# Linear attention in plain float32, its narrow products in 64- and 32-wide parts of TensorE, in a fused attention and gated-MLP kernel

## The chip, the cores and the metric

The program runs on one core of a Trainium2 chip. The time is device microseconds (us) of that core; each time given is the median over several executions, and the profile is of one further execution. The engines are called by the profile's names: PE is TensorE (PEld its weight loads), DVE is VectorE, ACT is ScalarE, POOL is GpSimd, SP is SyncE, which here issues every DMA.

## The reference

Eight batches of eight heads, 576 tokens, head size 64, 128 features. The attention is linear: no softmax over tokens, but a feature map and two products. Its output is the input of a gated MLP without a non-linearity.

```python
def phi(x):                                      # x: b h s d (8, 8, 576, 64)
    proj = np.einsum('bhsd,df->bhsf', x, w_phi)  # w_phi: 64 x 128
    proj = proj - np.max(np.abs(proj), axis=-1, keepdims=True)
    return np.concatenate([np.exp(proj), np.exp(-proj)], axis=-1)   # 256 features
q_p, k_p = phi(q), phi(k)
kv  = np.einsum('bhsf,bhsd->bhfd', k_p, v)
z   = np.sum(k_p, axis=2)
num = np.einsum('bhsf,bhfd->bhsd', q_p, kv)
den = np.einsum('bhsf,bhf->bhs', q_p, z)[..., None] + 1e-06
x   = num / den                                  # as 4608 tokens x 512
out = ((x @ w_a) * (x @ w_b)) @ w_out            # 512 -> 1536 -> 512
```

The MLP's weights arrive as float64 bits and are decoded on the chip.

## The kernel before, in words

**Two number formats.** PE multiplies float32 exactly but slowly, and `F32R`, a rounded float32, fast. Where the kernel wants both it splits a number into `hi + lo`, both F32R, and makes three products (`hi*hi`, `hi*lo`, `lo*hi`; helper `products`, L99). The MLP does this throughout. The attention does it from a certain head pair on; before that it uses plain float32 ("plain" in the code), with thresholds in L38: the k features are plain for the first 9 of 32 pairs, the q features for 2, the sums over k for 11, the numerators for 7.

**Attention.** A unit of work is a pair of heads (4 pairs per batch, 32 in all). Per pair:

- `k_load`, `rest_load` load k and v (512 of the 576 tokens in four chunks of 128; the last 64 tokens of two pairs share one 128-row "rest" tile), and where not plain split them: `ks` (k stacked as hi over lo), `vaug`/`vl`.
- `features` makes the k features for two chunks at a time: product `pk` (L219 plain, L228 split), maximum and subtraction on DVE, two exponentials on ACT, where split also `keh` (ACT) and `kel` (DVE).
- `kv_add` (L286) accumulates v-transposed times features into `kvps`, per chunk and head, 256 columns wide. v has a 65th column of ones, so that row 65 of the result is z. Split: three products, two of 65 and one of 64 weights' columns.
- `k_finish` transposes the result (`pt`, four transposes) into `kvh` (and `kvl`).
- `q_side`, once per head: load q, `pq` (L340) for its features, a maximum over partitions on POOL (`mb`), a subtraction on DVE, two exponentials on ACT, where split `qeh` (ACT) and `qel` (DVE), and `pn` (L364), whose 65 rows are numerator and denominator. They go to DRAM as `xun` and `den`; `reciprocals` turns `den` into `rec` once per batch.

**The MLP** has d_ff 1536 in two passes: pass 0 takes 6 of 12 slices of 128 for 16 blocks of 288 tokens, pass 1 the other 6 for 9 blocks of 512 tokens and adds the stored partial sums. `pa`, `pb` (L515) and `po` (L538) are its products, 216 matmuls per block. `decode` turns the raw weights `raw` into `wh`/`wl` with two ACT and six DVE instructions per weight tile (18 tiles for each pass) by way of two work tiles `wg`, `ws`.

**Order.** `attention_steps` places the stages of every pair in numbered turns (tables L24 to L31). After each turn `due` MLP steps are given out (L35); batch b's blocks may start `BLOCK_LAG` turns after its reciprocals. That is the order of writing; the framework's scheduler then settles the order on each engine. Each engine runs its list strictly in that order. Pass 1 follows when pass 0 is through.

Of the kernel before, what the change touches and what calls it, by code (L numbers as in the profile page):

```python
# [55 lines left out]
@with_exitstack
def tile_kernel(ctx, tc, qT, km, kr, vm, vr, w_phi, w_a, w_b, w_out, out):

# [40 lines left out]
    def products(a, b):  # L99

        if len(a) == 1:
            return [(a[0], b[0])]
        return [(a[0], b[0]), (a[0], b[1]), (a[1], b[0])]

    def attention_consts(a1):
# [18 lines left out]
        vaug = []  # L124
        for i in range(2):
            t = a1.tile([P, NFULL, 2, D + 1], F32R, name=f"vaug{i}")
            nc.vector.memset(t[:, :, :, D : D + 1].bitcast(F32), 1.0)
            vaug.append(t)
        return w2, wh, wl, wk32, wk2, ident, vaug

    def engine(step, b):
        return {"v": nc.vector, "s": nc.scalar}[ENGINES[step][min(b, 2)]]

    def copy(eng, dst, src):
        if eng is nc.scalar:
            eng.copy(dst, src)  # L136
        else:
            eng.tensor_copy(dst, src)

    def split(hi, lo, src, eng_hi, eng_lo):  # L140

        copy(eng_hi, hi, src)
        eng_lo.tensor_tensor(lo, src, hi, op=ALU.subtract)  # L143

    def stack(hi_lo, src, eng_hi, eng_lo):

        copy(eng_hi, hi_lo, src)
        eng_lo.tensor_tensor(hi_lo[D:], src[D:], hi_lo[D:], op=ALU.subtract)  # L148

    def k_load(b, pr, a1, a2, ps, consts, st):  # L150
        vaug = consts[-1]
        u = f"{b}_{pr}"
        i = b * NPAIR + pr
        n = NFULL * P
        if i < PLAIN_K:
            k32 = a1.tile([P, n], F32, tag="ks", bufs=2, name=f"k32_{u}")
            nc.sync.dma_start(k32, km[b, pr])
# [4 lines left out]
        if i < PLAIN_KV:  # L162
            v32 = a1.tile([P, NFULL, 2, D + 1], F32, tag="vl", bufs=2, name=f"v32_{u}")
            nc.vector.memset(v32[:, :, :, D : D + 1], 1.0)
        else:
            v32 = a1.tile([P, NFULL, 2, D], F32, tag="v32", name=f"v32_{u}")
        nc.sync.dma_start(v32[:, :, :, :D], vm[b, pr])
        yield
        st["k", b, pr] = (k32,)
        if i >= PLAIN_K:  # L170
            ks = a1.tile([P, 2, n], F32R, tag="ks", bufs=2, name=f"ks_{u}")
            stack(ks, k32, engine("k_hi", b), engine("k_lo", b))
            st["k", b, pr] = (ks,)
        yield
        st["v", b, pr] = (v32,)
        if i >= PLAIN_KV:
            va = vaug[pr % 2]
            vl = a1.tile([P, NFULL, 2, D + 1], F32R, tag="vl", bufs=2, name=f"vl_{u}")
            split(va[:, :, :, :D], vl[:, :, :, :D], v32, engine("v_hi", b), engine("v_lo", b))
            st["v", b, pr] = (va, vl)  # L180
        yield

    def rest_load(b, g, a1, a2, ps, consts, st):

        u = f"{b}_{g}"
        i = b * NPAIR + 2 * g
        if i < PLAIN_K:
            k32 = a1.tile([P, P], F32, tag="rk32", name=f"rk32_{u}")
            nc.sync.dma_start(k32, kr[b, g])
# [4 lines left out]
        v32 = a1.tile([P, 2, D + 1], F32, tag="rv32", name=f"rv32_{u}")  # L194
        nc.vector.memset(v32[:, :, D : D + 1], 1.0)
        nc.sync.dma_start(v32[:, :, :D], vr[b, g])
        yield
        st["rk", b, g] = (k32,)
        if i >= PLAIN_K:
            ks = a1.tile([P, 2, P], F32R, tag="rk", name=f"rk_{u}")  # L200
            stack(ks, k32, engine("k_hi", b), engine("k_lo", b))
            st["rk", b, g] = (ks,)
        yield
        st["rv", b, g] = (v32,)
        if i >= PLAIN_KV:
            vh = a1.tile([P, 2, D + 1], F32R, tag="rvh", name=f"rvh_{u}")
            vl = a1.tile([P, 2, D + 1], F32R, tag="rvl", name=f"rvl_{u}")
            split(vh, vl, v32, engine("v_hi", b), engine("v_lo", b))
            st["rv", b, g] = (vh, vl)
        yield  # L210

    def features(u, i, k_, c0, n, a2, ps, consts):

# [22 lines left out]
        plain = i < PLAIN_KV  # L236
        shape = [P, 2 * n, 2, F]
        if plain:
            e = a2.tile(shape, F32, tag=f"keh{n}", bufs=n, name=f"ke_{u}")
        else:  # L240
            e = a2.tile([P, 4, 2, F], F32, tag="ke", bufs=1, name=f"ke_{u}")[:, : 2 * n]
# [2 lines left out]
        es = (e,)
        if not plain:
            eh = a2.tile(shape, F32R, tag=f"keh{n}", bufs=n, name=f"keh_{u}")
            el = a2.tile(shape, F32R, tag=f"kel{n}", bufs=n, name=f"kel_{u}")
            split(eh, el, e, engine("ke_hi", i // NPAIR), nc.vector)
            es = (eh, el)
        yield es  # L250
# [23 lines left out]
    def rest_add(b, pr, st):  # L274
        rows = slice(pr % 2 * REST, (pr % 2 + 1) * REST)
        kv_add(b, pr, [v_[rows] for v_ in st["rv", b, pr // 2]], [e_[rows] for e_ in st["re", b, pr // 2]], st)
        yield

    def kv_add(b, pr, vs, es, st):

        left = st["kv_left", b, pr] = st["kv_left", b, pr] - 1
        for j in range(2):
            parts = products(vs, es)
            for n_, (v_, e_) in enumerate(parts):
                width = D if n_ == 2 else D + 1
                nc.tensor.matmul(  # L286
                    st["kv_ps", b, pr][:width, j],
                    v_[:, j, :width],
                    e_[:, j],
                    start=(left == NFULL and j == 0 and n_ == 0),  # L290
                    stop=(left == 0 and n_ == len(parts) - 1),
                    skip_group_check=True,
                )
# [5 lines left out]
    def k_finish(b, pr, a1, a2, ps, consts, st):  # L299
        ident = consts[5]  # L300
        u = f"{b}_{pr}"
        assert st["kv_left", b, pr] == 0
# [3 lines left out]
        pt = pool.tile([P, 4, P], F32, tag=tag, bufs=bufs, name=f"pt_{u}")
        for g in range(4):
            nc.tensor.transpose(pt[:, g, : D + 1], kvT[: D + 1, g, :], ident[: D + 1, : D + 1])
        plain = b * NPAIR + pr < PLAIN_NUM
        kvh = a2.tile([P, 4, D + 1], F32 if plain else F32R, tag="kvh", name=f"kvh_{u}")  # L310
        nc.scalar.copy(kvh, pt[:, :, : D + 1])
        st["kv", b, pr] = (kvh,)
        if not plain:
            kvl = a2.tile([P, 4, D + 1], F32R, tag="kvl", name=f"kvl_{u}")
            nc.vector.tensor_tensor(kvl, pt[:, :, : D + 1], kvh, op=ALU.subtract)
            st["kv", b, pr] = (kvh, kvl)
        yield

    def q_side(b, pr, j, a1, a2, ps, consts, st):
        w2, wh, wl = consts[:3]  # L320
        h = 2 * pr + j
        i = b * NPAIR + pr
        plain_q, plain = i < PLAIN_Q, i < PLAIN_NUM
        u = f"{b}_{h}"
# [311 lines left out]
```

## Time and profile before

| | |
|---|---|
| median of 3 runs | 1301.69 us (1298.23 to 1302.58) |
| the profiled execution | 1299.35 us, its span 1297.6 us |
| granted TensorE clock, mean | 0.991 |
| busy of the span: PE, PEld | 1253.2 us (97%), 1114.9 us (86%) |
| busy: DVE, ACT, POOL | 841.9 (65%), 703.1 (54%), 157.1 us (12%) |
| HBM | 138.8 MB in the DMA queue of the kernel, mean 108 GB/s |

How to read a row of a timeline: start in us from the span's start, duration in us, engine, line, operation, output<-inputs, weights' rows*columns, moving operand, and how many instructions are merged (x4); in brackets the idle time ahead and what ended it. The profile counts records: a plain float32 matmul leaves two, each with a weight load of its own, an F32R one leaves one. Matmuls overlap in their pipeline, so a record's duration is longer than its share of PE's time; the spacing of starts in an unbroken run is what one really costs.

### The profile page before, as it was taken

How to read it: one execution, taken by the hardware profiler on the slowest of the kernel's cores; microseconds unless marked ns; L12 is line 12 of the kernel's file. 1: busy time of each engine (PE TensorE's matmuls, PEld its weight loads, DVE VectorE, ACT ScalarE, POOL GpSimd, SP SyncE). 2: the span in 40 equal slices, each digit the busy share in tenths (PEclk: the TensorE clock that was granted, in tenths of full speed). 3: DMA queues.
4: the chain of work that ended last, by engine and by line, in shares of the span. 5: the costliest groups of instructions: out<-in, count | busy, mean ns of one | idle time of the engine just before them, and what ended most of it. 6: DMA issues, size and time to landing. Idle time of an engine off the chain costs nothing.

```text
span 1297.6 us, 20263 instructions
## 1 busy us (share of the span) xinstructions
PE 1253.2 (97%) x7632; PEld 1114.9 (86%) x7632; DVE 841.9 (65%) x1388; ACT 703.1 (54%) x1471; POOL 157.1 (12%) x70
## 2 busy tenths in 40 slices
PE   7989879999999999999999999999999999999998
PEld 4558659999999999999999899988888888888887
DVE  5999985798998989988973532698323323333322
ACT  5777775788989888988884322443211211211210
POOL 2323211131222222221220000000000000000000
PEclk9999979999999999999999999999999999999999
DMA  8666532443433435344224821243233133133100
GB/s 197 169 179 177 155 100 77 110 114 107 132 102 112 134 82 156 87 123 123 55 80 117 241 83 56 66 155 110 73 114 98 49 114 98 49 114 96 51 33 33
DMA packets 116594, 140.12 MB, mean 108 GB/s; under 512 B 29136, under 2 KB 81872, under 8 KB 116496
## 3 DMA queue, kind: packets, MB, share of 16 engines
q1 hardware_dynamic: 116496, 138.83, 37.4%
q8 instruction: 60, 0.98, 0.3%
q14 instruction: 38, 0.31, 0.1%
HBM read 110.18 MB, written 28.61 MB: 107 GB/s over the span
## 4 chain that ended last, share of the span: by engine, by line
PE 53%; DVE 7%; ACT 2%; issue 2%; DMA 2%; SPq 0%; DVEq 0%; ACTq 0%
PE po L538 17%; PE pb L515 16%; PE pa L515 16%; PE kvps L286 2%; PE pn L364 2%; DVE qs L148 1%; DVE kel L143 1%; DMA rb<-rec 1%; DVE qel L143 0%; DVE kd L231 0%; DVE kd L234 0%; DVE ks L148 0%; PE pq L340 0%; DMA den<-xn 0%; DVE x L492 0%
## 5 line engine op out<-in xcount | busy, mean ns | idle before, releaser
L344 POOL PARTITION_ALL_REDUCE mb<-p x64 | 156.4, 2444 | 512.8 <-ACT p L341 304.0
L515 PE MATMUL pa<-xh,wh_a 128*128 128x288 f32 (+1 forms) x600 | 200.2, 334 | 5.3 <-DVE h L520 3.1
L538 PE MATMUL po<-hh,wl_o 128*128 128x288 f32 (+1 forms) x600 | 195.8, 331 | 7.2 <-DVE wl_o L433 7.0
L515 PE MATMUL pb<-xh,wh_b 128*128 128x288 f32 (+1 forms) x600 | 198.8, 331 | 4.1 <-ACT h L519 4.1
L520 DVE TENSOR_TENSOR h<-pb,h 128x288 f32<-128x288 f32 (+1 forms) x150 | 80.5, 538 | 185.9 <-PE pb L515 185.2
L515 PE MATMUL pa<-xl,wh_a 128*128 128x288 f32 (+1 forms) x600 | 198.8, 331 | 0.0
L538 PE MATMUL po<-hl,wh_o 128*128 128x288 f32 (+1 forms) x600 | 198.2, 332 | 0.1
L515 PE MATMUL pb<-xl,wh_b 128*128 128x288 f32 (+1 forms) x600 | 198.0, 330 | 0.0
L515 PE MATMUL pa<-xh,wl_a 128*128 128x288 f32 (+1 forms) x600 | 197.8, 330 | 0.0
L515 PE MATMUL pb<-xh,wl_b 128*128 128x288 f32 (+1 forms) x600 | 197.4, 329 | 0.0
L538 PE MATMUL po<-hh,wh_o 128*128 128x288 f32 (+1 forms) x600 | 196.2, 333 | 1.0 <-ACT o L541 0.5
L136 ACT CAST hh<-h 128x288 fp32r<-128x288 f32 (+1 forms) x150 | 75.3, 502 | 192.5 <-DVE h L520 189.8
L519 ACT COPY h<-pa 128x288 f32<-128x288 f32 (+1 forms) x150 | 70.2, 469 | 186.3 <-PE pa L515 184.5
L538 PEld LDWEIGHTS po<-hh,wl_o 128*128 128x128 f32 x600 | 113.2, 189 | 16.6 <-DVE wl_o L433 7.3
L515 PEld LDWEIGHTS pa<-xh,wh_a 128*128 128x128 f32 x600 | 113.3, 189 | 15.8 <-DVE h L520 4.2
L515 PEld LDWEIGHTS pb<-xh,wh_b 128*128 128x128 f32 x600 | 112.9, 188 | 14.7 <-ACT h L519 5.9
L538 PEld LDWEIGHTS po<-hh,wh_o 128*128 128x128 f32 x600 | 112.8, 190 | 11.1 <-DVE h L520 0.9
L538 PEld LDWEIGHTS po<-hl,wh_o 128*128 128x128 f32 x600 | 113.9, 190 | 9.0 <-DVE hl L143 0.4
L515 PEld LDWEIGHTS pa<-xh,wl_a 128*128 128x128 f32 x600 | 113.6, 189 | 8.6
L515 PEld LDWEIGHTS pa<-xl,wh_a 128*128 128x128 f32 x600 | 113.4, 189 | 8.8 <-issue 0.2
L515 PEld LDWEIGHTS pb<-xl,wh_b 128*128 128x128 f32 x600 | 113.0, 188 | 8.5 <-issue 0.2
L515 PEld LDWEIGHTS pb<-xh,wl_b 128*128 128x128 f32 x600 | 112.9, 188 | 8.5
(131 smaller groups left out, 2339.2 us busy)
## 6 DMA issues: line engine op xcount, KB each, us to landing
q<-in_qT SPq DMA_DIRECT2D x124, 144.0 KB
k<-in_km SPq DMA_DIRECT2D x55, 256.0 KB
xun<-xn SPq DMA_DIRECT2D x64, 144.0 KB
x<-xun SPq DMA_DIRECT2D x32, 288.0 KB
rb<-rec SPq DMA_DIRECT2D x64, 144.0 KB
part<-o SPq DMA_DIRECT2D x16, 576.0 KB
o<-part SPq DMA_DIRECT2D x9, 1024.0 KB
v<-in_vm SPq DMA_DIRECT2D x32, 256.0 KB
```

The costliest lines, as they stand in the source:

```text
L136: eng.copy(dst, src)
L143: eng_lo.tensor_tensor(lo, src, hi, op=ALU.subtract)
L148: eng_lo.tensor_tensor(hi_lo[D:], src[D:], hi_lo[D:], op=ALU.subtract)
L286: nc.tensor.matmul(st["kv_ps", b, pr][:width, j], v_[:, j, :width], e_[:, j], start=(left == NFULL and j == 0 and n_ == 0), stop=(left == ...
L344: nc.gpsimd.partition_all_reduce(mb, p32, P, bass_isa.ReduceOp.absmax)
L364: nc.tensor.matmul(pn[: D + 1, :HALF], kv_[:, 2 * j + s, :], e_[:, s, tok], **at)
L515: nc.tensor.matmul(acc, w[:, cc * P : (cc + 1) * P], x, start=(k == 0), stop=(k == 3 * NCC - 1))
L519: nc.scalar.copy(h32, pab["a"])
L520: nc.vector.tensor_tensor(h32, pab["b"], h32, op=ALU.mult)
L538: nc.tensor.matmul(acc, w[:, cc * P : (cc + 1) * P], h, start=(k == 0), stop=(k == 3 * NFS[p] - 1))
```

## The change

- `kv_add`, `q_side` and `k_finish` use plain float32 for all pairs; `products`, the hi/lo copies of q, v and of the features, `vaug`, and the table `ENGINES` go. Only the k features stay split, from pair 7 on (before: 9).
- The sums over k: v has 64 columns now, head 0 of a pair goes to PSUM partitions 0 to 63, head 1 to 64 to 127 (columns 0 to 63 and 64 to 127 of the array). z is a product of its own: 32 columns of ones as weights, in one of four 32-column parts, `q = 2c + j`. So per two chunks four 64-column and four 32-column products, 256 columns of features each.
- `k_finish`: two 128-wide transposes, and two products with `pick`, which add up the z rows.
- `q_side` takes a pair at once: one load of 128 rows; `pq` with 64 rows of weights per head, rows 0 to 63 or 64 to 127; `pn` with 64 columns per head; the denominator `pd` as 32-column products, one part per head and half of the tokens.
- `decode`'s work tiles `wg`, `ws` have two buffers in pass 0 (before: one).
- The tables of turns and paces are others.

```diff
-TURNS0, TURNS, PAIRS0 = 5, 4, 7
+TURNS0, TURNS, PAIRS0 = 5, 4, 5
-KV_TURN = 7
-Q_TURNS, Q_STEP = (0, 3, 4, 6, 9), 3
-DECODE_TURN, BLOCK_LAG = 2, 8
-PACE0, PACE, PACE0_UNTIL = 0.65, 0.9, 18
-PLAIN_K, PLAIN_Q, PLAIN_KV, PLAIN_NUM = 9, 2, 11, 7
+KV_TURN = 8
+Q_TURNS = (0, 3, 4, 6, 7, 9, 11)
+DECODE_TURN, BLOCK_LAG = 2, 6
+PACE0, PACE, PACE0_UNTIL = 0.8, 0.9, 24
+PLAIN_K = 7
+QUAD = 32
...
+        ones = a1.tile([P, QUAD], F32, name="ones")
+        nc.vector.memset(ones, 1.0)
+        pick = a1.tile([P, 2, QUAD], F32, name="pick")
+        nc.vector.memset(pick, 0.0)
+        for q in range(4):
+            nc.vector.memset(pick[q * QUAD : q * QUAD + 1, q % 2], 1.0)
...
+        kv_add(b, pr, [(v[:, c0 + c, j], e[:, 2 * c + j], j, 2 * c + j) for c in range(2) for j in range(2)], consts, st)
...
+    def kv_add(b, pr, parts, consts, st, rows=slice(0, P)):
+        ones, ps = consts[4], st["kv_ps", b, pr]
         left = st["kv_left", b, pr] = st["kv_left", b, pr] - 1
-        for j in range(2):
-            parts = products(vs, es)
-            for n_, (v_, e_) in enumerate(parts):
-                width = D if n_ == 2 else D + 1
-                nc.tensor.matmul(st["kv_ps", b, pr][:width, j], v_[:, j, :width], e_[:, j], ...)
+        for i, (v_, e_, j, q) in enumerate(parts):
+            nc.tensor.matmul(ps[j * D : (j + 1) * D, 0], v_, e_.rearrange("p s f -> p (s f)"), **at)
+        for v_, e_, j, q in parts:
+            to = ps[q * QUAD : (q + 1) * QUAD, 1]
+            nc.tensor.matmul(to, ones[rows], e_.rearrange("p s f -> p (s f)"), tile_position=(rows.start, q * QUAD), **at)
...
+        q32 = a2.tile([P, S], F32, tag="q32", name=f"q32_{u}")
+        nc.sync.dma_start(q32, qT[b, 2 * pr : 2 * pr + 2].rearrange("j d s -> (j d) s"))
+        for i, tok in enumerate(toks):
+            pq = [ps.tile([P, 512], F32, tag="att", name=f"pq_{u}_{i}_{j}")[:, :HALF] for j in range(2)]
+            for j in range(2):
+                rows = slice(j * D, (j + 1) * D)
+                nc.tensor.matmul(pq[j], w2[rows], q32[rows, tok], start=True, stop=True)
...
+        for i, tok in enumerate(toks):
+            for s in range(2):
+                for j in range(2):
+                    nc.tensor.matmul(pn[i][j * D : (j + 1) * D], kv[:, s, j], es[j][:, s, tok], **at)
+        for s in range(2):
+            for j in range(2):
+                for i, tok in enumerate(toks):
+                    q = (2 * j + i) * QUAD
+                    at = dict(start=(s == 0), stop=(s == 1), tile_position=(0, q))
+                    nc.tensor.matmul(pd[q : q + QUAD], z[:, s, j], es[j][:, s, tok], **at)
...
-            return pool.tile(shape, dt, tag=kind, bufs=1, name=name)
+            return pool.tile(shape, dt, tag=kind, bufs=2, name=name)
```

Two places show how the instructions stand after scheduling. The first is PE in the middle of the program, where the products of a pair stand among those of the MLP. Before, a head's numerators (`qeh`, `qel` and `kvh`, `kvl` are the hi and lo halves of the q features and of the transposed sums):

```order
L340 MATMUL pq_0_1_3802<-qs_0_3794,wh 128x288
L340 MATMUL pq_0_1_3802<-qs_0_3794,wl 128x288
L364 MATMUL pn_5_0_3857<-qeh_5_3620,kvh_2_3474 65x288 x2
L364 MATMUL pn_5_0_3857<-qel_5_3621,kvh_2_3474 65x288 x2
L364 MATMUL pn_5_0_3857<-qeh_5_3620,kvl_2_3476 65x288 x2
L538 MATMUL po_3_1_4346<-hh_3_0_3751,wh_0_o 128x288
```

and in the changed program the denominators of a pair (`pd`, after its eight `pn`), two chunks of k sums (64 and 32 columns), the rest's sums (64 rows), and the next pair's q products:

```order
L308 MATMUL pd_2_4431<-qe_2_0_4097,kv_2_4253 32x288 x2
L308 MATMUL pd_2_4431<-qe_2_1_4308,kv_2_4253 32x288 x2
L233 MATMUL kvps_3_4311<-ke_3_2_4320,v_4_3_3756 64x256 x4
L237 MATMUL kvps_3_4311<-ke_3_2_4320,ones 32x256 x4
L233 MATMUL kvps_3_4311<-ke_1_r,rv_4_1_3485 64x256 x2
L237 MATMUL kvps_3_4311<-ke_1_r,ones 32x256 x2
L278 MATMUL pq_0_0_0_4466<-q_5_0_4273,w_100 128x288
L278 MATMUL pq_0_0_1_4467<-q_5_0_4273,w_100 128x288
L278 MATMUL pq_0_1_0_4472<-q_5_0_4273,w_100 128x288
L464 MATMUL pa_4_5_4488<-xh_4_0_4069,wh_5_a 128x288
```

The products of different parts now mostly stand behind one another, in runs of four to eight, and the runs of different width follow one another directly.

The second is DVE near the start, while weights are decoded (L427 to L433, later L376 to L382) beside the first pairs. Before:

```order
L427 TENSOR_SCALAR wg_2_a<-wg_2_a 128x512
L428 SCALAR_TENSOR_TENSOR ws_2_a<-raw_2_a,wg_2_a 128x512
L233 TENSOR_REDUCE m_3_2_599<-pk_3_2_596 128x4
L138 CAST qs_7_705<-q_0_7_631 128x576
L429 TENSOR_SCALAR wg_2_a<-ws_2_a 128x512
L234 TENSOR_TENSOR kd_3_2_595<-pk_3_2_596,m_3_2_599 128x512
L148 TENSOR_TENSOR qs_7_705<-q_0_7_631,qs_7_705 64x576
L345 TENSOR_TENSOR p_0_5_545<-p_0_5_545,mb_5_592 128x576
L431 SCALAR_TENSOR_TENSOR wg_2_a<-raw_2_a,wg_2_a 128x512
L432 TENSOR_TENSOR ws_2_a<-ws_2_a,wh_2_a 128x512
L433 TENSOR_TENSOR wl_2_a<-ws_2_a,wg_2_a 128x512
```

and now:

```order
L286 TENSOR_TENSOR p_0_2_1_492<-p_0_2_1_492,mb_2_1_626 128x576
L380 SCALAR_TENSOR_TENSOR wg_3_b<-raw_3_b,wg_3_b 128x512
L376 TENSOR_SCALAR wg_4_a<-wg_4_a 128x512
L191 TENSOR_REDUCE m_0_0_712<-pk_0_0_709 128x4
L381 TENSOR_TENSOR ws_3_b<-ws_3_b,wh_3_b 128x512
L377 SCALAR_TENSOR_TENSOR ws_4_a<-raw_4_a,wg_4_a 128x512
L192 TENSOR_TENSOR kd_0_0_708<-pk_0_0_709,m_0_0_712 128x512
L382 TENSOR_TENSOR wl_3_b<-ws_3_b,wg_3_b 128x512
L378 TENSOR_SCALAR wg_4_a<-ws_4_a 128x512
L380 SCALAR_TENSOR_TENSOR wg_4_a<-raw_4_a,wg_4_a 128x512
L381 TENSOR_TENSOR ws_4_a<-ws_4_a,wh_4_a 128x512
```

The q splits (L138, L148) are gone, and two weights (`3_b`, `4_a`) are decoded interleaved. Ahead of DVE's first MLP instruction (the first `x`, which releases the first `pa`) stand 9 finished weights before and 13 now; ahead of PE's first `pa` stand 200 attention matmuls before and 292 now.

More of the change, by code (lines that the diff above doesn't have):

```diff
@@ L97, in attention_pools @@
         return a1, a2, ps
[L99 to L103, printed above, removed]
     def attention_consts(a1):
@@ L123, in attention_consts, with stack, split @@
         make_identity(nc, ident)
[L124 to L148, printed above, removed]
+        ones = a1.tile([P, QUAD], F32, name="ones")
[4 more added lines that the diff above has]
+            nc.vector.memset(pick[q * QUAD : q * QUAD + 1, q % 2], 1.0)
+        return w2, wk32, wk2, ident, ones, pick
+    def stack(hi_lo, src):
+        nc.scalar.copy(hi_lo, src)
+        nc.vector.tensor_tensor(hi_lo[D:], src[D:], hi_lo[D:], op=ALU.subtract)
+    def split(hi, lo, src):
+        nc.scalar.copy(hi, src)
+        nc.vector.tensor_tensor(lo, src, hi, op=ALU.subtract)
     def k_load(b, pr, a1, a2, ps, consts, st):
-        vaug = consts[-1]
         u = f"{b}_{pr}"
-        i = b * NPAIR + pr
         n = NFULL * P
-        if i < PLAIN_K:
-            k32 = a1.tile([P, n], F32, tag="ks", bufs=2, name=f"k32_{u}")
-            nc.sync.dma_start(k32, km[b, pr])
+        plain = b * NPAIR + pr < PLAIN_K
+        if plain:
+            k_ = a1.tile([P, n], F32, tag="ks", bufs=2, name=f"k32_{u}")
+            nc.sync.dma_start(k_, km[b, pr])
         else:
@@ L161, in k_load @@
                 nc.sync.dma_start(k32[r * D : (r + 1) * D], km[b, pr].rearrange("(j d) s -> d j s", j=2))
[L162 to L167, printed above, removed]
-        yield
[L169 to L180, printed above, removed]
+        v32 = a1.tile([P, NFULL, 2, D], F32, tag="v32", bufs=3, name=f"v32_{u}")
+        nc.sync.dma_start(v32, vm[b, pr])
+        st["v", b, pr] = v32
+        yield
+        if not plain:
+            k_ = a1.tile([P, 2, n], F32R, tag="ks", bufs=2, name=f"ks_{u}")
+            stack(k_, k32)
+        st["k", b, pr] = k_
         yield
@@ L185, in rest_load @@
         u = f"{b}_{g}"
[L186 to L189, printed above, removed]
+        plain = b * NPAIR + 2 * g < PLAIN_K
+        if plain:
+            k_ = a1.tile([P, P], F32, tag="rk32", name=f"rk32_{u}")
+            nc.sync.dma_start(k_, kr[b, g])
         else:
@@ L235, in features @@
         yield
[L236 to L241, printed above, removed]
+        e = a2.tile([P, 2 * n, 2, F], F32, tag=f"ke{n}", bufs=1 + n, name=f"ke_{u}")
         nc.scalar.activation(e[:, :, 0, :], d, AF.Exp)
         nc.scalar.activation(e[:, :, 1, :], d, AF.Exp, scale=-1.0)
[L244 to L250, printed above, removed]
+        yield e
     def k_chunks(b, pr, c0, a1, a2, ps, consts, st):
         u = f"{b}_{pr}"
-        gen = features(f"{u}_{c0}", b * NPAIR + pr, st["k", b, pr][0], c0, 2, a2, ps, consts)
+        gen = features(f"{u}_{c0}", b * NPAIR + pr, st["k", b, pr], c0, 2, a2, ps, consts)
         yield next(gen)
-        es = next(gen)
+        e = next(gen)
         yield
@@ L305, in k_finish @@
         pool, tag, bufs = spare(b, ps)
[L306 to L316, printed above, removed]
@@ L317, in k_finish @@
-        yield
[L319 to L324, printed above, removed]
+        pt = pool.tile([P, 512], F32, tag=tag, bufs=bufs, name=f"pt_{u}")
+        for s in range(2):
+            nc.tensor.transpose(pt[:, s * P : (s + 1) * P], kvT[:, 0, s], ident)
+        nz = 2 * QUAD
+        for s in range(2):
+            to = pt[:, 2 * P + s * nz : 2 * P + (s + 1) * nz]
+            nc.tensor.matmul(to, kvT[:, 1, s], pick.rearrange("p j r -> p (j r)"), start=True, stop=True)
@@ L356, in q_side @@
-        yield
-        parts = [(s, kv_, e_) for kv_, e_ in products(st["kv", b, pr], es) for s in range(2)]
-        xn = a2.tile([P, S], F32, tag="xn", name=f"xn_{u}")
-        for i in range(2):
-            tok = slice(i * HALF, (i + 1) * HALF)
-            pn = ps.tile([P, 512], F32, tag="att", name=f"pn_{u}_{i}")
-            for n_, (s, kv_, e_) in enumerate(parts):
-                at = dict(start=(n_ == 0), stop=(n_ == len(parts) - 1))
-                nc.tensor.matmul(pn[: D + 1, :HALF], kv_[:, 2 * j + s, :], e_[:, s, tok], **at)
-            nc.scalar.copy(xn[: D + 1, tok], pn[: D + 1, :HALF])
```

151 lines of the change are left out of this document (67 added, 84 removed).

## The prediction

> **What bounds the kernel now.** I read the page's head and its shares of the engines, then busy time by stretches, then PE's timeline, because the spacing of starts there gives what each kind of product really costs.
>
> ```profile
> span 1297.6 us, 20263 instructions
> PE 1253.2 (97%) x7632; PEld 1114.9 (86%) x7632; DVE 841.9 (65%) x1388; ACT 703.1 (54%) x1471; POOL 157.1 (12%) x70
> 0.00:94.00 94.00, 78.06 (x340) 48.93 (x340) 76.92 (x139) 63.69 (x136) 29.22 (x18) 1.00 0.71 185
> 0.00:200.00 200.00, 169.36 (x849) 123.83 (x850) 170.94 (x298) 139.03 (x298) 52.43 (x27) 0.95 0.60 161
> 200.00:700.00 500.00, 493.03 (x3736) 477.56 (x3735) 430.63 (x672) 416.70 (x895) 104.65 (x43) 1.00 0.38 104
> 850.00:1298.00 448.00, 443.86 (x1967) 367.49 (x1966) 172.55 (x271) 98.86 (x165) 0.00 (x0) 1.00 0.27 84
> ```
>
> The columns of a stretch are its length, then busy time and records of PE, PEld, DVE, ACT, POOL, the granted clock, DMA share and GB/s. From 200 us on PE is busy throughout, with DVE and ACT at 86% and 83% in the stretch that holds most of the attention: PE's own work sets the time there, and time freed on DVE or ACT buys little. In the first 200 us PE is at 85% and the clock at 0.95; there the others set it. Now PE's spacings:
>
> ```profile
> 59.60 1.13 PE L364 MATMUL pn<-qe,kvh 128*65 128x288 f32 x4
> 60.57 1.03 PE L219 MATMUL pk<-wk,k 128*128 128x256 f32 x4
> 61.44 1.89 PE L286 MATMUL kvps<-ke,v 128*65 128x256 f32 x8
> 63.16 0.41 PE L308 MATMUL pt<-ident,kvT 65*128 65x65 f32 x4
> ...
> 167.45 3.62 PE L286 MATMUL kvps<-ke,v 128*65 128x256 f32 x16
> 170.99 1.08 PE L286 MATMUL kvps<-ke_r,rv 64*65 64x256 f32 x4
> 172.00 0.40 PE L340 MATMUL pq<-qs,wh 128*128 128x288 f32 x1
> 172.24 0.29 PE L340 MATMUL pq<-qs,wl 128*128 128x288 f32 x1
> ...
> 400.36 0.42 PE L364 MATMUL pn<-qeh,kvh 128*65 128x288 f32 x2
> ...
> 401.94 0.29 PE L515 MATMUL pb<-xh,wh_b 128*128 128x288 f32 x1
> 402.20 0.41 PE L308 MATMUL pt<-ident,kvT 65*128 65x65 f32 x4
> 402.42 0.38 PE L515 MATMUL pb<-xh,wl_b 128*128 128x288 f32 x1
> ...
> 409.47 0.28 PE L286 MATMUL kvps<-keh,vaug 128*65 128x256 f32 x1
> 409.59 0.28 PE L286 MATMUL kvps<-kel,vaug 128*65 128x256 f32 x1
> 409.70 0.28 PE L286 MATMUL kvps<-keh,vl 128*64 128x256 f32 x1
> 409.82 0.28 PE L286 MATMUL kvps<-keh,vaug 128*65 128x256 f32 x1
> ...
> 410.87 0.29 PE L340 MATMUL pq<-qs,wh 128*128 128x288 f32 x1
> ...
> 413.16 0.28 PE L286 MATMUL kvps<-keh,vl 128*64 128x256 f32 x1
> 413.37 0.33 PE L286 MATMUL kvps<-keh_r,rvh 64*65 64x256 f32 x1
> 413.54 0.27 PE L286 MATMUL kvps<-kel_r,rvh 64*65 64x256 f32 x1
> ...
> 414.01 0.27 PE L286 MATMUL kvps<-keh_r,rvl 64*64 64x256 f32 x1
> 414.21 0.40 PE L515 MATMUL pa<-xh,wh_a 128*128 128x288 f32 x1
> 414.45 0.30 PE L515 MATMUL pa<-xl,wh_a 128*128 128x288 f32 x1
> ```
>
> A plain record of 256 columns takes 1.72/8 = 0.215 (61.44 to 63.16) or 3.54/16 = 0.221 us (167.45 to 170.99), say 0.218; of 288 columns 0.97/4 = 0.2425. A plain product is two such records. Split, 256 columns take 1.40/12 = 0.117 us (409.47 to 410.87), 288 columns 1.58/12 = 0.132 (400.36 to 401.94). So today a plain product costs 0.44 or 0.485 us and three split ones 0.35 or 0.395: about the same. Whatever the change gains on PE must come from parts running at the same time, and nothing in this trace does that.
>
> **PE's work before.** The MLP: 1944 matmuls of 512 columns at 443.86/1967 = 0.2257 us and 3456 of 288 at 0.133 (the 3736 records of the second stretch average 0.134 with what is lost between them), 439 + 461 = 900. k sums: 224 plain records at 0.218 and 624 split at 0.117, 121.6. pq: 16 x 0.2425 + 240 x 0.133 = 35.9. pn: 112 x 0.2425 + 600 x 0.132 = 106.2. These narrow products make 263.7. pk: 82 x 0.218 + 206 split records, taken like those of the k sums, x 0.12 = 42.6. pt: 128 x 0.055 (402.20 to 402.42) = 7. Visits to 64 rows, priced below: 39 x 0.28 = 11. Together 1224 of 1297.6; 74 us are lost. Of these the first 94 us hold 24 (340 records are 70 us by these prices), the next 106 some 26, the rest 24.
>
> **The change, part by part.**
>
> *Narrow products.* The new program has 1280 records of 256 columns (half with 64, half with 32 columns of weights) and 1280 of 288 (256 pq, 512 pn, 512 pd). One after another they are 279 + 310 = 589 us. The bounds are this (no overlap) and all parts of a group at once: 640 v records in two parts 69.8, 512 ones in four 27.9, the rest's 128 ones in two 14.0, pq in two 31.0, pn in two 62.1, pd in four 31.0, together 236. I take 236, the lower bound, -28 us against 263.7: the weight loads in these rows already lie under running matmuls (PEld 86% beside PE 97%), the parts share no rows or columns of the array, and different PSUM partitions or banks take the results. It is a choice, not a reading, and the rivals are about it.
>
> *Seams.* Each run of parts starts and ends with one part alone, and PE's order mixes MLP matmuls in. None if runs overlap, up to half a record (0.11) for some ten runs a pair, 35 us; I take 10.
>
> *Visits to 64 rows.* Entering them costs (413.37 - 413.16) - 0.117 = 0.09 and 0.17 - 0.117 = 0.05, leaving 0.20 - 0.117 = 0.08 and 0.24 - 0.133 = 0.11: 0.33 a visit. In plain float32 it is 1.01 - 4 x 0.218 = 0.14 and 0.24 - 0.133 = 0.11, 0.25. I take 0.28. The new order has 95 visits (pq is one each time) for 39: +16, between -11 (the overlap swallows all) and +18.
> Narrower columns cost nothing: `vl` with 64 columns stands between two of 65 at the same 0.11 to 0.12 (409.59 to 409.82). The Trainium skill (TensorEngine Tiling (Array Packing), Key Properties) says that changing the tiling mode drains TensorE. The rows with 64 matmul rows agree, the 64-column row does not. By that rule all changes of shape would pay, 454 before and 476 now, so at half a visit, 0.14, this term would be +3 instead of +16, an estimate.
>
> *pk and pt.* Two more pairs split: 2 x (8 x 0.218 - 8 x 0.117) and a rest, -2. Two transposes of 128 instead of four of 65 columns, and two plain products of 64: about twice the 7 us, +7.
>
> *DVE, ACT, SP, POOL.* From 200 us on what goes there (the splits of q, of the features, of v) is off the path, and so are the fewer q loads on SP's queue and the halved stores. Its cover is PE's work: DVE and ACT would have to be late, and they get earlier. POOL's work stays. In the start it matters:
>
> ```profile
> L148 DVE TENSOR_TENSOR qs<-q,qs 64x576 fp32r<-64x576 f32 x18 | 16.6, 920 | 1.2 <-ACT qs L136 0.6
> L143 DVE TENSOR_TENSOR qel<-qe,qeh 128x1152 fp32r<-128x1152 f32 x5 | 6.7, 1350 | 0.0
> L431 DVE SCALAR_TENSOR_TENSOR wg_b<-raw_b,wg_b 128x512 f32<-128x512 uint32 x6 | 5.2, 866 | 0.1
> PE po L538 <- DVE wl_o L433: 7.0, 2, 4.8
> PE pk L219 <- DMA k<-in_km: 5.3, 1, 5.3
> ...
> 94.57 0.40 PE L515 MATMUL pa<-xh,wh_a 128*128 128x288 f32 x1 [1.69 <-ACT xh L136]
> ```
>
> Those are DVE's rows and PE's waits of the first 200 us, and PE's first `pa`. Ahead of the first MLP block DVE loses 9 qs (8 us) and 4 casts (2), and gains 4 weights, six instructions of 0.4 to 0.9 us each, about 4.2 a weight: 17. So the first `pa` comes some 7 to 9 us later, near 103. PE has 292 attention matmuls for that, which are 67 us if parts overlap: 36 lost there for 24. From there to 200 us DVE lacks the 17 us of weights and the rest of qs and qel, and with it the 7.0 us wait for `wl_o`: I put 10 lost for 26. After 200 us the waits for splits go, 14 for 24. Together 60 for 74, -14; bounds -45 (DVE's 23 us and all waits gained) and +10 (the first `pa` late, nothing won back).
>
> **Sum.** -28 + 10 + 16 - 2 + 7 - 14 = -11 on the span of 1297.6: 1286.6. The profiled execution took 1299.35, 1.75 more than its span, and the median of the runs shown is 2.3 above that: **1290 us**, 0.9% faster. Its own range, from the terms' bounds, is 1262 to 1306.
>
> **Rivals.**
>
> *Only neighbours overlap* (slower). A plain product is two records on the same part. If PE starts matmuls strictly in order, the second record holds up the next part until the first is through; then the end of one product runs beside the start of the next, two at a time, however many parts there are. The two-part groups lose nothing, ones and pd get a factor of two for four: 589/2 = 295, +31 for -28, and seams of 35. More PE work at the start means less lost there (38 for 74). 31 + 35 + 16 - 2 + 7 - 36 = +51: **1352 us**. For it: in the trace every start follows the one before, and both records of a product always stand together. Against: no row shows a second part being held up. The point that decides: the change loses unless the 589 us are compressed by 2.4 (263.7 + 2 - 7 - 16 - 10 + 14 = 246.5).
> The Trainium skill (TensorE: Matmul & The Clock Gate, Packing small matmuls) states that matmuls start and end strictly in program order, and that four row parts ran 3.07 and three column parts 2.38 times as fast. The order rule is this rival. With the measured shares (0.78 of the ideal, an estimate for two parts) the narrow products would be 302 us and the time about 1335, the same side. No run here shows either.
>
> *Nothing overlaps* (slower). 589 - 264 = +326, with the other terms and 36 less lost time +326 - 2 + 7 + 16 - 36 = +311: **1613 us**. The trace has no two parts side by side, so it cannot exclude it.
>
> *The start gains much more* (faster). DVE is busy 171 of the first 200 us; if its 23 us come straight off and the visits to 64 rows are hidden, lost time halves (-37), visits cost +0 and seams 5: -28 + 5 - 2 + 7 - 37 = -55, **1246 us**. Against it: four more weights stand ahead of the first block.
>
> **How the numbers follow.** All parts at once 0.50, only neighbours (or the measured shares) 0.31, the start gains more 0.12, nothing overlaps 0.07. 0.3%, about 4 us, is what a measurement of this kernel can tell. Faster: three quarters of the first case and the third, 0.50. Same: 0.07. Slower: 0.43. The range 1252 to 1362 holds the first case, nearly all of the second and a part of the third, about 0.85; the likeliest alone is 1262 to 1306.
>
> **What would show it.** In the timeline after, the spacing of a run of kvps with 64 columns: 0.11 per record if two parts run together, 0.22 if not; with ones and of pd 0.055 to 0.06 if four run, 0.11 if neighbours, 0.22 if none. PE's first `pa` near 103 us. DVE's busy time below 655 us, since these three rows alone, 187 us of 842, have no successor:
>
> ```profile
> L143 DVE TENSOR_TENSOR qel<-qe,qeh 128x1152 fp32r<-128x1152 f32 x50 | 68.7, 1374 | 20.5 <-ACT qeh L136 18.4 <-PE pq L340 2.1
> L148 DVE TENSOR_TENSOR qs<-q,qs 64x576 fp32r<-64x576 f32 x60 | 65.2, 1086 | 9.6 <-ACT qs L136 8.0
> L143 DVE TENSOR_TENSOR kel<-ke,keh 128x1024 fp32r<-128x1024 f32 x42 | 52.8, 1258 | 0.6 <-ACT keh L136 0.4
> ```
>
> A visit to 64 rows for pq, about 0.25 beyond its records. The prediction is wrong if four parts need 0.11 per record, or if PE waits for ACT or POOL in the middle, where I have put nothing.

## The result: 2.3% slower, and the profile after

The changed kernel takes 1330.75 us (median, 1330.57 to 1333.05), the kernel before on the same chip 1300.97: a ratio of 1.0235, 95% interval 1.0214 to 1.0257. The forecast was 1290.

The head of the page and the stretches that were shown of before. In a stretch the columns are length, busy time and records of PE, PEld, DVE, ACT, POOL, granted clock, DMA share, GB/s:

```profile
span 1328.8 us, 21126 instructions
PE 1311.0 (99%) x8440; PEld 1026.6 (77%) x8440; DVE 638.7 (48%) x1155; ACT 579.8 (44%) x1262; POOL 144.0 (11%) x70
0.00:94.00 94.00, 86.91 (x550) 42.56 (x550) 84.11 (x146) 65.81 (x136) 29.80 (x18) 1.00 0.62 194
0.00:200.00 200.00, 189.24 (x1310) 115.97 (x1312) 154.56 (x277) 134.81 (x294) 53.17 (x28) 0.99 0.50 152
200.00:700.00 500.00, 497.42 (x3814) 362.92 (x3811) 237.69 (x448) 288.72 (x669) 90.83 (x42) 1.00 0.34 100
850.00:1298.00 448.00, 448.00 (x2084) 376.66 (x2083) 189.87 (x311) 110.50 (x191) 0.00 (x0) 1.00 0.28 88
```

Everything that the change freed is there to see: DVE fell from 841.9 to 638.7 us, in the middle stretch from 430.63 to 237.69, and PE hardly waits any more, not even in the first 200 us (189.24 busy for 169.36). Yet the span grew by 31.2 us: PE itself has more to do. Its timeline in the steady part shows what (start, duration, line, operation, weights' rows*columns, moving operand, merged records; MLP rows left out):

```profile
435.44 2.16 PE L301 MATMUL pn<-qe,kv 128*64 128x288 f32 x16
437.53 1.18 PE L308 MATMUL pd<-qe,kv 128*32 128x288 f32 x16
438.64 1.08 PE L233 MATMUL kvps<-ke,v 128*64 128x256 f32 x8
439.65 0.64 PE L237 MATMUL kvps<-ke,ones 128*32 128x256 f32 x8
440.22 0.65 PE L233 MATMUL kvps<-ke_r,rv 64*64 64x256 f32 x4
440.80 0.62 PE L237 MATMUL kvps<-ke_r,ones 64*32 64x256 f32 x4
441.35 0.76 PE L278 MATMUL pq<-q,w 64*128 64x288 f32 x4
442.04 0.40 PE L464 MATMUL pa<-xh,wh_a 128*128 128x288 f32 x1
442.28 0.30 PE L464 MATMUL pa<-xl,wh_a 128*128 128x288 f32 x1
...
442.76 0.75 PE L278 MATMUL pq<-q,w 64*128 64x288 f32 x2
443.44 0.40 PE L464 MATMUL pa<-xl,wh_a 128*128 128x288 f32 x1
```

The parts do run side by side. Eight v records take 1.01 us from start to start; in two parts, at 0.218 a record, they should take 0.872. Eight ones records in four parts take 0.57 for 0.436, pn 2.09 for 1.94, pd 1.11 for 0.97. Each of these runs is its ideal plus about 0.14 us, whatever its length. The four-record pq run takes 0.69 for 0.485 (+0.2), and a run of two pq records, one product without a partner, takes 0.68 too: there the second part stands idle.

Adding the spacings of starts (less the idle time ahead) for every line gives the accounts in us, before and after. Idle time here and below is PE's waits of over 0.15 us, without the first load's:

| PE's time | before | after | difference |
|---|---|---|---|
| sums over k (`kvps`) | 129.0 | 85.5 + 57.1 | +13.5 |
| `pq` | 42.8 | 63.2 | +20.4 |
| `pn`, `pd` | 112.0 | 72.6 + 39.3 | 0 |
| `pt` | 8.4 | 7.2 + 12.5 | +11 |
| `pk` | 45.2 | 50.2 | +5 |
| the MLP | 915.8 | 923.2 | +7.3 |
| idle | 34.9 | 9.0 | -26 |

Together they make the measured 31.2. The MLP's matmuls are the same; those that follow a narrow run start late (442.04 to 442.28 is 0.24, where the next ones need 0.133).

### The profile page after: what moved, and what is told of

The parts are those of the page before. It is cut to its first block, busy times and chain, and to the rows that moved or that the text cites. A ratio compares the mean times of both kernels' runs of the same rounds, so it can differ in the third digit from the quotient of the medians.

```text
span 1328.8 us, 21126 instructions
## 1 busy us (share of the span) xinstructions
PE 1311.0 (99%) x8440; PEld 1026.6 (77%) x8440; DVE 638.7 (48%) x1155; ACT 579.8 (44%) x1262; POOL 144.0 (11%) x70
## 4 chain that ended last, share of the span: by engine, by line
PE 92%; DMA 3%; DVE 2%; SPq 1%; issue 1%; ACT 0%; DVEq 0%; ACTq 0%
PE pa L464 22%; PE pb L464 22%; PE po L487 22%; PE kvps L233 6%; PE pn L301 5%; PE pq L278 4%; PE kvps L237 4%; PE pd L308 3%; PE pk L186 2%; DMA rb<-rec 1%; PE pt L257 1%; DMA x<-xun 1%; PE pk L177 1%; PE pt L253 1%; DMA raw_a<-in_w_a 0%
## 5 line engine op out<-in xcount | busy, mean ns | idle before, releaser
L285 POOL PARTITION_ALL_REDUCE mb<-p x64 | 143.3, 2239 | 490.4 <-ACT p L280 356.9
L487 PEld LDWEIGHTS po<-hh,wh_o 128*128 128x128 f32 x600 | 112.0, 188 | 15.6 <-issue 6.3
L487 PEld LDWEIGHTS po<-hl,wh_o 128*128 128x128 f32 x600 | 112.6, 188 | 12.5 <-issue 2.4
```

The costliest lines, as they stand in the source:

```text
L285: nc.gpsimd.partition_all_reduce(mb, p32[j], P, bass_isa.ReduceOp.absmax)
L487: nc.tensor.matmul(acc, w[:, cc * P : (cc + 1) * P], h, start=(k == 0), stop=(k == 3 * NFS[p] - 1))
```

## The experiments

**The theory.** Parts overlap in full, but each run of another shape of weights costs PE a fixed 0.13 to 0.2 us, and the new order has 528 such runs (counted in PE's order by rows x columns of the weights and number format, the full-array runs between the narrow ones included, names with one shape together; 619 if names are told apart). At 0.14 that is 74 us. Rivals: the parts overlap badly; the order within a run holds parts up; other engines make the narrow products late.

**Shapes by themselves (e4).** Not this computation: 19 sequences of products on the same small tiles, in program order, with nothing else running.

> Not the computation: runs of matmuls of given shapes on resident data, one after another, with no waits; its output is not the reference's. Read by the spacing of starts. Theory (parts run side by side, every run of a new shape pays a fixed piece): plain, 256 columns, one 64-column part 0.218 us a record, two parts 0.109, four 32-column parts 0.055, whatever the order within the run; four products of 64 columns and four of 32 in turn 0.872 + 0.436 + 2 x 0.135 = 1.58 us a cycle; a single 64-row product among split ones costs its 0.485 and about 0.3. Rival (only neighbours overlap): four 32-column parts 0.109 a record, the cycle near 1.9 us, and two or four products of one part in a row lose the overlap. A second question is which changes are free: split products of 64 among those of 128 columns (expected free, as in the trace of before), plain ones of 128 after split ones of 128 (open).

It ran once, 177.7 us. Rows of its timeline (three 512-column records separate the sequences):

```profile
19.55 7.12 PE L36 MATMUL bank<-x,w 128*64 128x256 f32 x32
26.61 0.97 PE L36 MATMUL bank<-xr,wr 128*128 128x512 f32 x3
27.50 5.40 PE L36 MATMUL bank<-x,w 128*64 128x256 f32 x48
32.83 0.98 PE L36 MATMUL bank<-xr,wr 128*128 128x512 f32 x3
33.74 5.45 PE L36 MATMUL bank<-x,w 128*64 128x256 f32 x48
39.12 0.97 PE L36 MATMUL bank<-xr,wr 128*128 128x512 f32 x3
40.02 6.54 PE L36 MATMUL bank<-x,w 128*64 128x256 f32 x48
46.49 0.96 PE L36 MATMUL bank<-xr,wr 128*128 128x512 f32 x3
47.38 3.66 PE L36 MATMUL bank<-x,w 128*32 128x256 f32 x64
50.97 0.96 PE L36 MATMUL bank<-xr,wr 128*128 128x512 f32 x3
51.86 3.73 PE L36 MATMUL bank<-x,w 128*32 128x256 f32 x64
55.52 0.97 PE L36 MATMUL bank<-xr,wr 128*128 128x512 f32 x3
56.42 12.74 PE L36 MATMUL bank<-x,w 128*64 128x256 f32 x128
69.09 0.98 PE L36 MATMUL bank<-xr,wr 128*128 128x512 f32 x3
69.99 1.08 PE L36 MATMUL bank<-x,w 128*64 128x256 f32 x8
71.01 0.74 PE L36 MATMUL bank<-xr,wr 128*128 128x256 f32 x4
71.68 1.08 PE L36 MATMUL bank<-x,w 128*64 128x256 f32 x8
...
84.04 1.89 PE L36 MATMUL bank<-x,w 128*128 128x256 f32 x8
85.58 0.82 PE L36 MATMUL bank<-xr,wr 128*128 128x256 f32 x4
86.24 1.89 PE L36 MATMUL bank<-x,w 128*128 128x256 f32 x8
```

One 64-column part costs 7.06/32 = 0.221 us a record. Two in turn cost 5.33/48 = 0.111, two products of each in turn 0.112, four of each 0.135: the order matters only in long blocks on one part. Four 32-column parts in turn cost 3.59/64 = 0.056, two of each in turn 0.057. So the rival that the parts overlap badly does not hold, nor does the one on the order within a run; and as nothing else runs here, other engines have no part in what follows. Then the changes: eight cycles of four 64-column and four 32-column products take 12.67 us, 1.584 a cycle for 0.872 + 0.436, that is 0.138 for each of the two changes. A cycle of four 64-column and four full split products takes 1.69 (69.99 to 71.68) for 0.872 + 0.468: 0.35 for going and coming back. With full-width plain products in place of the narrow ones the cycle takes 2.20 (84.04 to 86.24) for 1.744 + 0.468 = 2.21: the number format alone costs nothing.

Two more readings of this trace bear on the cause. In another sequence four products on one 64-column part, where nothing overlaps, stand between four full split products:

```profile
149.52 1.94 PE L36 MATMUL bank<-x,w 128*64 128x256 f32 x8
...
152.07 1.94 PE L36 MATMUL bank<-x,w 128*64 128x256 f32 x8
```

The cycle takes 2.55 for 1.744 + 0.468, so going and coming back costs 0.34 again. The cost is not that a run begins and ends with one part alone. The weight loads (PEld) show what is held up, first at a change that costs, then at the free one:

```profile
72.16 0.14 PEld L36 LDWEIGHTS bank<-x,w 128*64 128x64 f32 x2
72.69 0.30 PEld L36 LDWEIGHTS bank<-xr,wr 128*128 128x128 f32 x2 [0.39 <-issue]
...
85.12 0.41 PEld L36 LDWEIGHTS bank<-x,w 128*128 128x128 f32 x2
85.55 0.41 PEld L36 LDWEIGHTS bank<-xr,wr 128*128 128x128 f32 x2
```

In the middle of a run a load starts about 0.002 us after the start of the product before it and lies under that product. So it does at 85.55 (the product before it starts at 85.550), where only the number format changes. From 64 columns to the full array the last narrow products start at 72.38, but the next load not before 72.69, together with its own product; PEld stood idle for 0.39 us. In the changed kernel, too, the last `v` products of the run above start at 439.34 and the first load for `ones` at 439.65. So at a change that costs, the next weights are not loaded ahead; why they are held back, no trace here shows.

**Fewer and more runs, the same work (e5, e6).**

```diff
 e5, k_chunks:                                  # once per pair, not per two chunks
-  kv_add(b, pr, [... for c in range(2) for j in range(2)], ...)
+  if len(es) == NFULL // 2:
+      kv_add(b, pr, [... for c0, e in es for c in range(2) for j in range(2)], ...)
 e6, kv_add:
-  four v products; four ones products
+  two v products; four ones products; two v products
```

> The changed kernel, except that the sums over k of a pair's two main chunks are issued together: eight v products, then eight ones products, where there were two times four and four. The work is the same; in PE's order there are 524 runs of one shape for 619. Theory 'each run of a new shape costs a fixed 0.13 to 0.2 us': 95 fewer runs are -12 to -19 us, so 1312 to 1319 for the changed kernel's 1330.8. Rival 'the parts themselves overlap badly, runs cost nothing': the same time, 1329 to 1333. Rival 'later sums make their readers late': slower than 1333, with idle time of PE ahead of the transposes.

> The changed kernel, except that each group of k sums is issued as two v products, four ones products, two v products (before: four, four). Same work, and every run still has enough parts to fill the array's columns. In PE's order there are 652 runs of one shape for 619. Theory 'a fixed 0.13 to 0.2 us a run': +4 to +7 us, 1335 to 1338, and the v rows of two products near 0.44 + 0.15 = 0.58 us apart from the next. Rival 'runs cost nothing': 1329 to 1333.

e5 takes 1316.87 us (ratio to before 1.0124, 1.0105 to 1.0144), e6 1336.86 (1.0282, 1.0264 to 1.03): -13.9 and +6.1 against the changed kernel, as the fixed cost has it. Counted by shapes of weights, e5 has 412 runs and e6 583 for 528. PE's time without idle moved by -19.5 us for 116 runs fewer, 0.17 each, and by +6.6 for 55 more, 0.12 each; in e5 idle time gave 6.0 back. A group of e6:

```profile
390.09 0.65 PE L234 MATMUL kvps<-ke,v 128*64 128x256 f32 x4
390.68 0.64 PE L241 MATMUL kvps<-ke,ones 128*32 128x256 f32 x8
391.25 0.65 PE L234 MATMUL kvps<-ke,v 128*64 128x256 f32 x4
391.83 0.40 PE L469 MATMUL pa<-xh,wh_a 128*128 128x288 f32 x1
```

The v products take 0.59 + 0.58 = 1.17 us for the 1.01 of one run of eight. The products are the same in all three kernels and only their grouping was edited. With e4, where nothing else runs, the fixed cost is shown.

**The pt term (e7).** The products with `pick` become two more transposes, and DVE adds the halves:

```diff
-  nc.tensor.matmul(to, kvT[:, 1, s], pick...)
+  nc.tensor.transpose(pt[:, (2 + s) * P : (3 + s) * P], kvT[:, 1, s], ident)
...
+  nc.vector.tensor_tensor(z[:, :, 0], z[:, :, 0], z[:, :, 1], op=ALU.add)
```

> The changed kernel, except that the sums of the features are transposed like the rest (two more transposes) and their two halves added by DVE, in place of the products with `pick`. Runs of one shape: 615 for 619. The four records of pick take 0.366 us, two more transposes should take 2 x 0.055 = 0.11: 32 x 0.25 = -8 us, 1323. Rival 'the longer way over ACT and DVE makes pd late': PE waits for DVE ahead of pn or pd, and the time is 1331 or above.

1323.72 us (1.0179, 1.016 to 1.0198), -7.0. The second line of `pt` fell from 12.5 to 5.8 us, idle time rose by 1 to 10.0.

**q as before (e1, e2, e8).** From pair 2 on (e1), `pq` is again two split products of 128 rows, with q stacked by ACT and DVE; e2 adds e5's edit; e8 does it from pair 8 on.

```diff
+  stack(qs, q32[j])
+  nc.tensor.matmul(pq_, wh, qs[:, tok], start=True, stop=False)
+  nc.tensor.matmul(pq_, wl, qs[:, tok], start=False, stop=True)
```

> The changed kernel with the q features made as before again, from pair 2 on: q split into hi and lo, F32R, two products of 128 rows per half and head; everything else as changed. Theory (each change of the array's shape costs PE a fixed piece, and pq changes it most often): in the changed trace pq takes 63.2 us of PE in some 80 runs, 39 of them a single product of 0.68 us beside no partner; split it is 240 x 0.133 + 4 = 36 us, and the MLP's slow restarts after pq go (some 6 us): -33 us, 1295 to 1302 us, about the time of the kernel before. Rival (the time is lost elsewhere, or the q splits on DVE and ACT become the bound again): 1325 us or more.

> As e1_q_split, and both groups of two chunks are added to the sums over k in one go: one run of eight 64-column products and one of eight 32-column ones per pair instead of two and two of four. Theory (a fixed piece of about 0.135 us per run): 32 pairs x 2 runs fewer = 64 x 0.135 = -8.6 us against e1, 1287 to 1294 us. Rival (the piece is paid per record or the later sums make the numerators late): no gain against e1, or slower.

> The changed kernel, except that from pair 8 on (first experiment: from pair 2 on) the features of q are two split products of 128 rows for one plain product of 64 rows. In the first experiment q's products fell by 0.64 us a pair, but the kernel got slower. Theory 'that loss was the start's: stacking q on ACT and DVE in the first 150 us': with the start left alone 24 x 0.64 = -15 us remain, and 40 more runs of one shape in PE's order (659 for 619) cost +5 to +8, so 1320 to 1325, with PE at 136 us or more busy in the first 150. Rival 'the loss is the order's in the steady part: k sums in more, shorter runs': 1331 to 1338.

e1 was a miss: 1339.73 us (1.0306, 1.028 to 1.0331), slower than the changed kernel, although `pq` fell from 63.2 to 44.1. e2 was one too: 1337.93 (1.0286, 1.0268 to 1.0304), no real step from e1. e8 takes 1317.18 (1.0134, 1.0111 to 1.0157), a little better than expected. The first 150 us of the changed kernel, e1 and e8, in this order:

```profile
0.00:150.00 150.00, 139.24 (x922) 80.36 (x923) 130.21 (x232) 105.15 (x226) 42.14 (x23) 0.99 0.57 174
...
0.00:150.00 150.00, 125.05 (x835) 74.67 (x836) 133.86 (x232) 104.50 (x218) 39.83 (x22) 0.93 0.60 176
...
0.00:150.00 150.00, 139.57 (x930) 81.55 (x931) 131.55 (x232) 105.41 (x226) 42.25 (x23) 0.99 0.57 174
```

With q stacked from pair 2 on, PE gets 835 records in for 922, is busy 14 us less, and is granted a clock of 0.93. The 14 us are waits: PE's idle time in e1 is 25.2 us, 19.6 of them in the first 150 us, where the changed kernel has 5.6. The longest (what waited, for what: us in total, times, longest) are for ACT's copy of the transposed sums and DVE's stacking of q:

```profile
PE kvps L233 <- ACT kv L259: 6.7, 2, 3.5
PE pq L297 <- DVE qs L121: 4.9, 2, 3.0
```

So the time is as e1's rival had it, and its second reason, DVE and ACT late with the q splits in the start, fits these waits. e8 leaves the start alone and has the gain: `pq` 63.2 to 45.4. Of these 17.8 us the sums over k take back 8.0, in more and shorter runs. For e1 not all is explained: beside the 16 us of idle time its sums over k grew by 17 us, and its runs by shape are no more (523).

**The decoder's second buffer (e3).** `bufs=1` for `wg` and `ws`.

> The changed kernel with one buffer for each of the decoder's two work tiles, as before. Theory (in the start DVE's amount of work counts, not the decoder's buffers): the same within 5 us, 1328 to 1336 us. Rival (the second buffer is what filled PE's first 200 us, where waiting fell from 35 to 10 us): 15 to 25 us slower, 1345 to 1355.

1329.87 us (1.0228, 1.0207 to 1.0249): it does nothing.

**The order tables alone (e9), on the kernel before.**

```diff
-TURNS0, TURNS, PAIRS0 = 5, 4, 7
+TURNS0, TURNS, PAIRS0 = 5, 4, 5
-DECODE_TURN, BLOCK_LAG = 2, 8
-PACE0, PACE, PACE0_UNTIL = 0.65, 0.9, 18
+DECODE_TURN, BLOCK_LAG = 2, 6
+PACE0, PACE, PACE0_UNTIL = 0.8, 0.9, 24
```

> The kernel before with the changed kernel's order tables alone: PAIRS0 5, BLOCK_LAG 6, PACE0 0.8 until turn 24. It tells where the 25 us of PE's idle time went that the change removes. Theory 'freed DVE and ACT': with DVE busy 171 of the first 200 us already, the tables alone move waits and give nothing: 1298 to 1306, PE's idle time near 35 us. Rival 'the order tables': PE's idle time falls by 15 to 25 us, 1276 to 1286.

1292.17 us (0.9936, 0.9911 to 0.9961): faster than both kernels, and between the two expectations. Idle time fell by 3.6 us only, from 34.9 to 31.3; the rest came off the MLP's spacings (915.8 to 910.7). So of the change's 26 us of idle time these tables can claim about 4. That the rest goes with the work that left DVE and ACT is not shown: PE's own work also grew by 57 us (1253.3 to 1310.7 without idle), which leaves the others more time to be ready, and in e11 below, where PE works 41 us less, idle time is back at 19.7.

**Visits to 64 rows in the kernel before (e10, e12).** From pair 12 on, the last 64 tokens' products use 128 rows of weights, half of them zero. In e10 the two groups of weights share their tiles, so a product may be taken with the next group's v (its time is read, not its output); e12 has new tiles for each group and e9's tables.

```diff
-  vh = a1.tile([P, 2, D + 1], F32R, tag="rvh", ...)
-  split(vh, vl, v32, ...)
+  vh = a1.tile([P, 2, 2, D + 1], F32R, tag="rvh", ...)      # zero in the other half
+  for p in range(2):
+      split(vh[rows, p], vl[rows, p], v32[rows], ...)
...
-  kv_add(b, pr, [v_[rows] for v_ in vs], [e_[rows] for e_ in es], st)
+  kv_add(b, pr, [v_[:, pr % 2] for v_ in vs], es, st)
```

> The kernel before, except that from pair 12 on the products over the last 64 tokens use 128 rows, the other half of their weights being zero (two more small copies and subtractions a group of two pairs), so that they are no visits to 64 rows. Theory 'a change of shape costs a fixed time, a full-row product of the same columns nothing more': 20 visits at 0.33 us are saved, -6.6 us, 1294. Rival 'the visits are hidden': 1300 to 1302.

> The kernel before with the changed kernel's order tables (e9) and with products of 128 rows, half of them zero, in place of the 20 visits to 64 rows (e10, here with new weights for every group, their zero halves set by POOL). In e10 the k sums and the q products after them took 7.5 us less of PE, but PE waited 5.8 us longer and the second product of the MLP took 3.4 more. Theory 'the visits cost 0.33 us each, and what they save is lost only where the order is tight': -3 to -7 us from e9's 1292.2, 1285 to 1289. Rival 'what PE saves comes back as waits, as in e10': 1291 to 1294.

The fixed time is gone from the rows; the timeline of e10:

```profile
414.86 0.28 PE L294 MATMUL kvps<-keh_r,rvh 128*65 128x256 f32 x1
...
415.44 0.28 PE L294 MATMUL kvps<-keh_r,rvl 128*64 128x256 f32 x1
415.56 0.30 PE L523 MATMUL pa<-xh,wl_a 128*128 128x288 f32 x1
415.69 0.30 PE L523 MATMUL pa<-xh,wh_a 128*128 128x288 f32 x1
```

Six records in 0.70 us, 0.117 each, and the MLP goes on at once, where before the visit cost 0.33 more. PE's k sums and q products take 4.8 us less in the whole of e10, but the MLP 3.7 more, and idle time rose by 2.8 to 37.7 (the 7.5 and 5.8 us that e12's expectation names come from waits of e10 that were counted twice). e10 takes 1299.69 us (0.9985, 0.9967 to 1.0003) and e12 1294.91 (0.9943, 0.9925 to 0.9962), not faster than e9: both miss what was expected. In e12 k sums of 125.4 for 129.6 stand beside 2.2 us more in the MLP and 2.0 more of idle time than in e9. So the visits do cost PE time, but what they save does not shorten these kernels; it comes back in the MLP and as waits.

**All together (e11).** e5, e7, e8 and one decode buffer in the changed kernel, and the last 64 tokens' products of 128 rows, joined to the group of the others:

```diff
+  parts += [(v[:, p, j], e[:, j], j, j, half[:, p]) for j in range(2)]   # half, v: zero in the other pair's rows
+  kv_add(b, pr, parts, consts, st, ps)
```

> The changed kernel with fewer runs of one shape: k sums of a pair in one group (as in e5), sums of the features transposed (e7), q split from pair 8 on (e8), the last 64 tokens' products made of 128 rows with zeros in the other half, so that they join that group, and one buffer for decoding. In PE's order there are 355 runs of one shape of weights, where the changed kernel has 528, e5 412 and e8 486. Theory 'a run costs a fixed time', by e5 (116 runs for 13.9 us) 0.12 each: from e8's 1317 -16 for 131 runs and -6 for the rest of pick, 1295, within 0.5% of the kernel before. Rival 'each edit alone helped by what it freed elsewhere': they do not add, 1305 to 1317.

1301.37 us (1.0005, 0.9989 to 1.0022): level with before. PE's time without idle fell by 26.0 us from e8, 5.5 of them in `pt`: 0.16 for each of the 131 runs saved. But idle time rose from 10.7 to 19.7, and so the time lies between the two expectations: on PE the edits add, and 9 us of it came back as waits. The longest of them, after the first load (what waited, for what: us in total, times, longest):

```profile
PE po L510 <- DVE wl_o L405: 4.1, 3, 2.1
PE kvps L238 <- ACT ke L204: 3.7, 3, 2.4
PE pa L487 <- DVE h L492: 2.9, 2, 2.0
```

The grouped sums wait for a pair's features, and the decoded weights are late again.

## Why the prediction was wrong

The measured 1330.75 us lies inside the range of 1252 to 1362, but outside the likeliest part, 1262 to 1306, and on the wrong side of the kernel before. That the range holds it is owed to a rival whose cause is wrong. By its own steps, on the span (+31.2 measured, -11 predicted):

- **Narrow products, "all parts at once".** The choice was right: e4 shows spacings of 0.111 with two parts and 0.056 with four, as "what would show it" asked, also with two products of each part in turn. (In the kernel they are 0.126 and 0.071, with each run's fixed cost in them.) The rival "only neighbours overlap" (1352) and the estimate with parts at 0.78 of their ideal (1335) had nearly the right time and the wrong cause: two parts ran 1.99 times as fast as one (0.221 to 0.111), four 3.9 times (to 0.056). The Trainium skill (TensorE: Matmul & The Clock Gate, Part 3: Packing small matmuls) has matmuls start and end strictly in order; if that holds here, it costs these products nothing.
- **Seams and visits are the failed step.** I took 10 us for seams, by half a record at ten runs a pair, allowed none to 35, and priced 95 visits to 64 rows at 0.28, but nothing for changes of columns. The argument was the row `vl`, where 64 columns stand free between two of 65. Those products are split ones at the first columns; the row says nothing on plain parts of 64 and 32 columns. Measured, any change to or between such parts costs 0.14 to 0.2 us: 528 runs, 74 us, for the 10 + 27 taken. In the account the narrow products took 317.7 us, 82 above the 236 of full overlap. Nor is the cost a seam of parts that overlap: in e4 a run in one part alone pays it too. Neither of the two signs of being wrong that were named came, and neither was about such changes. The sentence on the Trainium skill's rule priced all changes at 0.14 but charged the kernel before with 454 of them; those changes of columns and format there turned out free. The Trainium skill (TensorEngine Tiling (Array Packing), Key Properties) says that a change of tiling mode drains TensorE: e4 and e6 fit that, with 0.12 to 0.14 a change. The Trainium skill (TensorE: Matmul & The Clock Gate, Single matmul latency) gives a constant of about 166 ns, beside the streaming of the columns, for a single bf16 product at full clock; the 0.14 to 0.2 here are near it. The held-back weight loads of e4 fit a drain too, but that it is the cause is not shown.
- **pq.** Two parts at once were taken for all. In the order, 40 of its 72 runs hold a single product, whose partner stands elsewhere, at 0.68 each, as much as a pair takes. Instead of 31 us and its visits `pq` took 63.2. e8 shows that this is worth 17.8 us on PE.
- **Together** the narrow products went up by 33.8 us, where the terms -28, +10 and +16 had -2.
- **pt** +11 for +7, **pk** +5 for -2; e7 shows most of `pt`. For `pk` no run tells; its split records take 0.141 us each for 0.126 before.
- **The MLP** was left out of the sum and went up by 7.3, where its restarts after narrow runs are seen in the rows; e5 took 8 off it.
- **Lost time** -26 for -14, inside its bounds. Of the 74 us called lost, PE's waits are 34.9 and the 5.3 of the first load; the rest are products that cost more than their price (the MLP 915.8 for 900). The first `pa` came at 98.20 for 94.57, not at 103. From 150 to 680 us PE waits for nothing; after that three waits for DVE and ACT are left, 3.4 us. DVE's 638.7 us are below the 655 named.

## What to carry to other kernels

Count the changes of PE's tile shape before packing narrow products into parts: here each costs a fixed 0.12 to 0.2 us (e4, e5, e6), so a run must save that much, and work of one shape belongs together (e5: -14 us for issuing the same main products in half as many groups). A part without its partner gains nothing, and a schedule that mixes other work in will separate them. A row that shows a shape change to be free says so only for its own shapes and number format.

## What the runs showed that was not expected

Plain float32 products of the full array between split ones cost no change at all (2.20 us a cycle for 2.21), nor do split products of 64 columns in the first column part: in e4, sequences that mix them with full ones run at 0.129 us a record (113 records in 14.56 us, separators of 512 columns included). The fixed cost belongs to plain parts of the columns and to visits to part of the rows. Products of 128 rows of which half are zero cost PE no more than those of 64 rows (0.117 us a record in both), so padding with zeros is a way out of a visit.

And the tables that came with the change make the kernel before 0.6% faster, while the change, which has them, costs 2.3%. Against the kernel before with the same tables it is 3.0% (1.0235 / 0.9936). The best kernel of the study is the kernel before with the new tables, 1292.2 us.
